# Moving w_out's weight conversion from the attention to the matrix groups, and batching the softmax sums by three

## Chip, cores and metric

One core of one Trainium2 chip. The metric is the device time of one execution, in microseconds. Three runs of the kernel before took 563.81, 565.52 and 565.93 us, median 565.52.

## What is computed

Attention with a relative bias, then a layer of three matrix products with an elementwise maximum, and an output product. 4 batches, 8 heads, 576 positions, 64 columns a head; 2304 tokens, 512 columns, 768 hidden columns.

```python
scores = scale * q @ k.T + bias[head, i, j]
attn = exp(scores - max(scores)); attn = attn / (sum(attn) + 1e-9)
x = (attn @ v) as 2304 x 512
h = maximum(maximum(x @ w1, x @ w2), x @ w3)     # 512 x 768 each
out = h @ w_out                                   # 768 x 512
```

The reference's `moe` weights are float64: each weight reaches the chip as two 32-bit words, and the kernel makes float32 of them.

## The kernel before, in words

**Bias** (lines 93 to 180): a table of biases is made and written to DRAM; the attention reads it back per head pair and tile of rows.

**Attention** (class `Attention`, loop at line 1197 of the program). 16 units (head pair and batch) make 8 pairs of units, and each pair has nine steps, so there are 72 steps; `sched` is the order of the transposes, `fronts` that of the scores (the same but for the first pair, in which the fourth tile is scored sixth). A step's number modulo nine is called its place. `step(n)` issues, in this order: the scores of step n on TensorE (`front`, 12 matmuls of 288 columns in float32r, of two heads side by side); one to three pairs of output products (`pv`); on VectorE one `shift` per head (line 285: scores and bias, scale, and the row's minimum as negative maximum); on ScalarE one exponential per head with the row's sum (line 298), and an addition of 1e-9 to the two sums (line 302); VectorE's copies of finished outputs (line 402); the stream's VectorE token; then `norm(n-1)`: a reciprocal on VectorE (line 307) and the normalisation of both heads on GpSimd (line 310); `flip(n-5)`: the transposes of the step five back on TensorE (line 337), whose results ScalarE (lines 428, 429) and VectorE (line 431) copy out; the splits of the next units' queries and keys into a high and a low part (ScalarE line 239, GpSimd line 242). The score banks are two buffers, so a front waits for the shifts of the step before it. Engines run in the order in which the program issues.

**The stream of conversions** (`first`, lines 1103 to 1165; `convert`, line 540). One conversion makes 128 x 512 float32 of the word pairs: one operation on ScalarE (line 545) and four on VectorE (lines 547, 549, 552, 555). It is a generator of tokens, "scalar" or "vector"; from step 8 on each step but those at place 0 lets it do one VectorE token (two at places 1 and 3) and, at the step's end, one ScalarE token if that is next. Converted in this stream are sets 3 and 2 of the first three weights (each set two conversions), then w_out's three blocks (two conversions each, tiles `w64o` and `wao`), then sets 0 and 1. Sets 3, 2 and w_out's blocks get four GpSimd sums each and are written to `w_d` in DRAM with their sums, two stores of 512 KB a block. All loads and stores are on SP's queue, one after the other. A second stream (`early_x`) prepares parts of x from step 36 on.

**Matrix stage** (`moe`). First a plain stage for set 0, then groups 3 to 26: eight sets of weights by three column blocks, seven products a group (a Strassen-like scheme). Set s works in groups 3s to 3s+2. Products are made in the order p5, p6, p2, p7, the next group's p1, p4, p3; ahead of each there is a slot, 0 to 6, in which the jobs placed by `at(group, slot, ...)` are issued. ScalarE copies p1, p6 and p7 out of the bank in which the next product goes on; VectorE makes the sums of p2, p7 and p3 and, except in every third set, a running maximum of 128 x 384 and one of 128 x 1152 a group. Sets 4 to 8 are converted here, one token a job (`advance`), ten tokens in three groups from group 4 on. `raise_w` and `lower_w` split the weights on ScalarE and GpSimd. Groups 27 to 35 are the output products; their weights `wop` are loaded from `w_d` at groups 21 to 23 (`load_wo`, line 812) and split by `raise_wo` (ScalarE, line 827; the first of them, p3, in group 22, slot 2) and `lower_wo`.

Of the kernel before, what the change touches and what calls it, by code (L numbers as in the profile page):

```python
# [9 lines left out]
F32 = mybir.dt.float32  # L10
F32R = mybir.dt.float32r
U32 = mybir.dt.uint32
ACTF = mybir.ActivationFunctionType
ALU = mybir.AluOpType
# [5 lines left out]
def kernel(  # L20
# [12 lines left out]
    nc = tc.nc  # L33
# [10 lines left out]
    KFF = DFF // 128  # L44
# [152 lines left out]
    NS = len(STEPS)  # L197
# [2 lines left out]
    fronts = [sched[x] for x in (0, 1, 2, 4, 5, 3)] + sched[6:]  # L200
    NSTEP = len(sched)
    LAG = 5
    EB = LAG + 2
    GW = 128 * 2

# [3 lines left out]
    class Attention:  # L209
        def __init__(self, pool):  # L210
            self.pool = pool
            self.data = {}
            self.st = {}
            self.et = {}
            self.pvq = []
            self.done = []
            bias_t.extend(pool.tile([128, 2, S], F32, name=f"bias{t}", bufs=1) for t in range(NTQ + 1))
            self.vl = [pool.tile([128, 2, D], F32, name=f"vl{x}", bufs=1) for x in range(2)]
            for x in self.vl:
                nc.gpsimd.memset(x, 0.0)  # L220
# [70 lines left out]
        def expo(self, n, h):  # L291
            pool, st = self.pool, self.st[n]
            if h == 0:
                st["e"] = pool.tile([128, 2 * S], F32, tag=f"e{sched.index(fronts[n]) % (LAG + 1)}", bufs=1,
                                    name=f"e{n}")
                st["sm"] = pool.tile([128, 2], F32, tag="sm", bufs=EB, name=f"sm{n}")
            sn, nm = st.pop(h)
            nc.scalar.activation(st["e"][:, S * h:S * h + S], sn, ACTF.Exp, scale=-1.0, bias=nm,  # L298
                                 accum_out=st["sm"][:, h:h + 1])
            if h:  # L300
                sm = st["sm"]
                nc.scalar.activation(sm, sm, ACTF.Copy, bias=1e-9)

        def norm(self, n):
            st = self.st[n]
            rc = self.pool.tile([128, 2], F32, tag="rc", bufs=EB, name=f"rc{n}")
            nc.vector.reciprocal(rc, st["sm"])  # L307
            for h in range(2):
                e = st["e"][:, S * h:S * h + S]
                nc.gpsimd.tensor_scalar(out=e, in0=e, scalar1=rc[:, h:h + 1], scalar2=1.0,  # L310
                                        op0=ALU.mult, op1=ALU.mult)

        def group(self, un, g):
# [90 lines left out]


        def step(self, n, more=()):
            m, f = n - 1, n - LAG
            if n < NSTEP:
                pair, y = fronts[n]
                which, t = step_of(pair, y)  # L410
# [83 lines left out]
    def arith(eng, out, a, b, op=ALU.subtract):  # L494
        f = lambda x: x.bitcast(F32) if x.dtype == F32R else x
        eng.tensor_tensor(out=out, in0=f(a), in1=f(b), op=op)  # L496
# [37 lines left out]
    def fetch(pool, srcs, name):  # L534
        w = pool.tile([128, 512, 2], U32, tag="w64", bufs=2, name=f"w64{name}")
        n = 512 // len(srcs)
        for x, src in enumerate(srcs):
            nc.sync.dma_start(out=w[:, n * x:n * x + n].rearrange("p (c f) t -> p c (f t)", c=src.shape[1]), in_=src)
        return w

    def convert(pool, w, out, name):
        a = pool.tile([128, 512], F32, tag="wa", bufs=1, name=f"wa{name}")
        high, low, t = w[:, :, 1], w[:, :, 0], a.bitcast(U32)
        yield "scalar"
        nc.scalar.activation(a, high.bitcast(F32), ACTF.Abs, scale=2.0 ** 16)
# [46 lines left out]
    def moe(pool, wpool, x0, xa, xb, raw, sr):  # L592
# [89 lines left out]
        def at(n, k, *what):  # L682
            jobs.setdefault((n, k), []).extend(what)
# [84 lines left out]
        sumgen = {}  # L768

        fetched = {}  # L770

        def get(s, d):
            fetched[s, d] = fetch(wpool, w_srcs(s, d), f"{s}_{d}")

        def work_w():
            for s in range(4, NSET):
                made_w[s] = [raw_tile(pool if s % 2 == 0 else wpool, s), None]
                for d in range(2):
                    if d == 0:
                        get(s, 1)  # L780
                    elif s + 1 < NSET:
                        get(s + 1, 0)
                    yield from convert(wpool, fetched.pop((s, d)),
                                       made_w[s][0][:, 512 * d:512 * d + 512].bitcast(U32), f"{s}_{d}")

        ww = work_w()
        started = []
# [4 lines left out]
            next(ww, None)  # L792

        at(2, 0, F(get, 4, 0))
        for s in range(4, NSET):
            n = 3 * s - 8
            for k in range(10):
                at(n + (0, 0, 0, 0, 1, 1, 1, 2, 2, 2)[k], (2, 4, 5, 6, 2, 4, 6, 2, 4, 6)[k], advance)

        wo = {}  # L800
        wst = {}
# [222 lines left out]
    with tc.manual_schedule():  # L1024
# [45 lines left out]

        def first():
            todo = [(w_srcs(s, d), f"{s}_{d}") for s in PARK for d in range(2)]
            todo += [(wo_srcs(i + d * KFF // 2), f"o{i}_{d}") for i in range(KFF // 2) for d in range(2)]
            todo += [(w_srcs(s, d), f"{s}_{d}") for s in range(2) for d in range(2)]
            ahead = [fetch(wpool, *todo.pop(0))]

# [35 lines left out]

            for _ in range(2):
                yield "vector"
            parked = [(f"{s}", s - PARK[1]) for s in PARK] + [(f"o{i}", 2 + i) for i in range(KFF // 2)]
            for name, k in parked:
                made, half = block(name)
                for d in range(2):
# [47 lines left out]
        while n < NSTEP + LAG:  # L1166
            more = []
            if n >= NS - 1 and n % NS:
                more += [w0] * (2 if n % NS in (1, 3) else 1)
            if n >= 36 and n % NS in (3, 7, 8):  # L1170
                more.insert(0, ex)
            if n >= NSTEP + 1:
                more.insert(0, lx)
            at.step(n, more)
            n += 1
# [61 lines left out]
```

## Time and profile before

| | |
|---|---|
| median of three runs | 565.52 us |
| the profiled execution | 564.47 us, its span 562.70 us |
| busy in the span | TensorE 538.5 us (96%), VectorE 448.5 (80%), ScalarE 367.6 (65%), GpSimd 284.1 (50%) |
| bias table, first steps | to about 76 us |
| attention steps 9 to 71 | 75.85 to 276.30 us |
| last transposes, x's parts | to about 300 us |
| matrix groups and output | 300 to 562.7 us |
| granted TensorE clock | 1.00 in all slices (2.4 GHz) |
| DMA | 80.75 MB, SP's queue 45.2% of the 16 engines' span |

In a view of windows a line gives the window, its length, then for PE (matmuls), PEld (weight loads), DVE (VectorE), ACT (ScalarE) and POOL (GpSimd) the busy time with the number of instructions, then the granted clock, the DMA's busy share and GB/s. In a timeline a line gives start and duration in us, engine, line of the code, operation, result and operands, and in brackets the engine's idle time before it with what ended it.

### The profile page before, as it was taken

The numbers are of one execution on the slowest core, as the hardware profiler recorded it, in microseconds if no ns is written. First come the engines' busy times: TensorE is split into PE (matmuls) and PEld (weight loads), VectorE is DVE, ScalarE is ACT, GpSimd is POOL, SyncE is SP. The second block draws the span as 40 slices with busy tenths as digits, with TensorE's granted clock in tenths as the row PEclk, the third lists the DMA queues.
The fourth block names the chain that finished last, engine by engine and source line by source line (L and its number), as shares of the span: only waits on it lengthen the run. The fifth ranks groups of instructions, "written<-read, shape, count | busy, mean of one in ns | idle before, by whom it ended". The sixth has DMA issues, their size and how long they took to land.

```text
span 562.7 us, 13799 instructions
## 1 busy us (share of the span) xinstructions
PE 538.5 (96%) x5239; PEld 443.6 (79%) x5239; DVE 448.5 (80%) x949; ACT 367.6 (65%) x850; POOL 284.1 (50%) x296
## 2 busy tenths in 40 slices
PE   8999899999999899999889999999999999999997
PEld 4455666666666666666569999999999999999997
DVE  7996779999999999999668786754776237798883
ACT  6997798989899888898756643234323334445552
POOL 0637577788787989787620136344364242600000
PEclk9999999999999999999999999999999999999999
DMA  4895963944694457431200422421125300557552
GB/s 137 230 336 169 365 199 99 363 134 162 183 337 139 147 143 215 153 101 23 61 1 1 150 67 76 147 91 44 47 94 167 123 29 29 166 179 211 176 169 76
DMA packets 73170, 80.75 MB, mean 144 GB/s; under 512 B 23120, under 2 KB 54096, under 8 KB 73104
## 3 DMA queue, kind: packets, MB, share of 16 engines
q1 hardware_dynamic: 72960, 79.58, 45.2%
q8 instruction: 41, 0.67, 0.5%
q10 hardware_dynamic: 144, 0.29, 0.2%
q14 instruction: 25, 0.20, 0.1%
HBM read 50.61 MB, written 28.99 MB: 141 GB/s over the span
## 4 chain that ended last, share of the span: by engine, by line
PE 68%; ACT 13%; DVE 10%; issue 4%; DMA 2%; POOL 1%; SPq 0%; ACTq 0%; DVEq 0%; POOLq 0%
PE p L606 10%; PE p L604 10%; PE p L605 10%; ACT e L298 6%; PE pv L383 6%; PE bp L134 5%; PE s L275 5%; DVE sn L285 4%; PE p_o L950 4%; PE p_o L949 4%; PE p_o L948 4%; ACT et L428 2%; PE tp L337 2%; DVE et L431 2%; PE c L604 2%
## 5 line engine op out<-in xcount | busy, mean ns | idle before, releaser
L310 POOL TENSOR_SCALAR e<-e,rc 128x576 f32<-128x576 f32 x144 | 112.8, 796 | 40.4 <-DVE rc L307 37.3
L298 ACT ACTIVATE e<-sn,nm 128x576 f32<-128x576 f32 x144 | 111.4, 774 | 23.1 <-DVE nm L285 21.6
L285 DVE CUSTOM_DVE_ANT_0 sn<-s,bias 128x576 f32<-128x576 f32 x144 | 102.7, 748 | 11.9 <-PE s L275 8.9
L383 PE MATMUL pv<-et,vt 128*64 128x320 f32 (+1 forms) x496 | 74.0, 418 | 3.9 <-ACT et L428 2.2
L496 POOL TENSOR_TENSOR wl<-wr,wh 128x256 fp32r<-128x256 f32 x25 | 23.0, 946 | 94.2 <-ACT wh L692 94.2
L275 PE MATMUL s<-kh,qh 64*128 64x288 f32 x256 | 58.5, 337 | 5.5 <-DVE nm L285 4.7
L431 DVE COPY et<-tp 128x512 f32<-128x512 f32 x72 | 48.4, 672 | 10.7 <-PE tp L337 5.7
L337 PE MATMUL tp<-ident,e 64*128 64x64 f32 x1152 | 55.4, 226 | 0.5 <-DVE et L431 0.4
L383 PEld LDWEIGHTS pv<-et,vt 128*64 128x64 f32 x496 | 32.4, 136 | 27.1 <-issue 6.7
L644 ACT COPY u<-p 128x384 f32<-128x384 f32 x24 | 11.5, 479 | 59.3 <-PE p L606 59.1
L275 PE MATMUL s<-kl,qh 64*128 64x288 f32 x256 | 49.2, 303 | 0.0
L337 PEld LDWEIGHTS lp<-ident,e 64*128 64x128 f32 x144 | 19.7, 137 | 36.6 <-issue 17.3
L275 PE MATMUL s<-kh,ql 64*128 64x288 f32 x256 | 46.3, 290 | 0.9 <-POOL ql L242 0.9
L428 ACT COPY et<-tp 128x512 f32<-128x512 f32 x72 | 41.2, 572 | 7.7 <-PE lp L337 5.3
L337 PEld LDWEIGHTS tp<-ident,e 64*128 64x128 f32 x1152 | 45.3, 139 | 0.9 <-DVE et L431 0.9
L242 POOL TENSOR_TENSOR kl<-kr,kh 128x576 fp32r<-128x576 f32 x16 | 36.5, 2280 | 16.6 <-ACT kh L239 16.5
L275 PEld LDWEIGHTS s<-kh,qh 64*128 64x128 f32 x256 | 35.2, 186 | 12.0 <-DVE nm L285 9.6
L134 PE MATMUL bp<-hid,w2s 128*32 128x79 f32 (+51 forms) x640 | 41.9, 406 | 2.5 <-DVE hid L113 1.4
L113 DVE TENSOR_SCALAR hid<-sm,bp 128x528 f32<-128x528 f32 (+17 forms) x108 | 41.4, 458 | 0.0
L337 PE MATMUL lp<-ident,e 64*128 64x64 f32 x144 | 35.4, 246 | 5.2 <-ACT et L429 5.0
L134 PEld LDWEIGHTS bp<-hid,w2s 128*32 128x32 f32 x640 | 20.6, 114 | 24.3 <-issue 16.8
L496 POOL TENSOR_TENSOR wl<-ws,wh 128x256 fp32r<-128x256 f32 x28 | 27.5, 1008 | 14.6 <-ACT wh L694 11.9
(230 smaller groups left out, 1650.5 us busy)
## 6 DMA issues: line engine op xcount, KB each, us to landing
bias_d<-bs SPq DMA_DIRECT2D x36, 295.5 KB, 5.5
bias<-bias_d SPq DMA_DIRECT2D x16, 576.0 KB, 6.6
w<-in_moe_w_dram SPq DMA_DIRECT2D x36, 256.0 KB, 3.5
h_d<-ht SPq DMA_DIRECT2D x18, 384.0 KB, 3.7
hin<-h_d SPq DMA_DIRECT2D x16, 384.0 KB, 4.6
qr<-in_qd_dram SPq DMA_DIRECT2D x16, 288.0 KB, 4.9
kr<-in_kd_dram SPq DMA_DIRECT2D x16, 288.0 KB, 5.2
vt<-in_v_dram SPq DMA_DIRECT2D x32, 128.0 KB, 3.6
```

The lines of the kernel that those rows point to most:

```text
L134: nc.tensor.matmul(bp[32 * c:32 * c + 32, o:o + w], lhsT=w2s, rhs=src, start=True, stop=True)
L275: nc.tensor.matmul(ss[h][:, x, 0:HALF], lhsT=u[q][p, 128 * t:128 * t + 128], rhs=u[k][p, cols], start=(j == 0), stop=(j == 2))
L285: nc.vector.tensor_tensor_reduce(out=sn.rearrange("p (a b) -> p a b", a=2), in0=st["s"][h][:, :, 0:HALF], in1=bt.rearrange("p (a b) -> p a ...
L298: nc.scalar.activation(st["e"][:, S * h:S * h + S], sn, ACTF.Exp, scale=-1.0, bias=nm, accum_out=st["sm"][:, h:h + 1])
L310: nc.gpsimd.tensor_scalar(out=e, in0=e, scalar1=rc[:, h:h + 1], scalar2=1.0, op0=ALU.mult, op1=ALU.mult)
L337: return nc.tensor.transpose(to, e2[p, k0:k0 + 128], ident[p, p])
L383: nc.tensor.matmul(pv[p], lhsT=w, rhs=x, start=(c == 0), stop=(c == NTQ))
L428: nc.scalar.copy(*tp0[0])
L431: nc.vector.tensor_copy(*x)
L604: nc.tensor.matmul(o, lhsT=hi[:, c], rhs=h[:, j], start=first and j == 0, stop=False, **on)
L605: nc.tensor.matmul(o, lhsT=hi[:, c], rhs=l[:, j], start=False, stop=False, **on)
L606: nc.tensor.matmul(o, lhsT=lo[:, c], rhs=h[:, j], start=False, stop=last and j == 1, **on)
```

## The change

w_out's blocks leave the attention's stream. In the matrix stage the conversions come in one order, set 4's two halves, w_out's first half-block, set 5's two, and so on, the last two of w_out at the end, one conversion a group from group 4 to 19 (w_out's in groups 6, 9, 12, 15, 18, 19), one token in each of slots 1, 2, 4, 5 and 6. The four sums of a block follow in the next group on GpSimd, with four stores in place of two. In the attention the stream gets one VectorE token a step at every place but 0. The sums of three steps share one tile, one addition and one reciprocal, so normalisation n is issued in step n+3 in place of n+1.

```diff
+    BATCH = 3
 def expo(self, n, h):
-                st["sm"] = pool.tile([128, 2], F32, tag="sm", bufs=EB, name=f"sm{n}")
+                if n % BATCH == 0:
+                    self.sm = pool.tile([128, 2 * BATCH], F32, tag="sm", bufs=3, name=f"sm{n}")
             sn, nm = st.pop(h)
+            x = 2 * (n % BATCH) + h
             nc.scalar.activation(st["e"][:, S * h:S * h + S], sn, ACTF.Exp, scale=-1.0, bias=nm,
-                                 accum_out=st["sm"][:, h:h + 1])
-            if h:
-                sm = st["sm"]
-                nc.scalar.activation(sm, sm, ACTF.Copy, bias=1e-9)
+                                 accum_out=self.sm[:, x:x + 1])
+            if x == 2 * BATCH - 1:
+                nc.scalar.activation(self.sm, self.sm, ACTF.Copy, bias=1e-9)
+                self.sums.append(self.sm)
 def norm(self, n):
-            rc = self.pool.tile([128, 2], F32, tag="rc", bufs=EB, name=f"rc{n}")
-            nc.vector.reciprocal(rc, st["sm"])
+            if n % BATCH == 0:
+                self.rc = self.pool.tile([128, 2 * BATCH], F32, tag="rc", bufs=3, name=f"rc{n}")
+                nc.vector.reciprocal(self.rc, self.sums.pop(0))
 def step(self, n, more=()):
-            m, f = n - 1, n - LAG
+            m, f = n - BATCH, n - LAG
...
 in moe:
+        order = []
+        for s in range(4, NSET):
+            order += [(s, 0), (s, 1), ("o", s - 4)]
+        order.append(("o", NSET - 4))
+            if d % 2 == 0:
+                stage[d // 2] = [pool.tile([128, 768], F32, tag="st", bufs=3, name=f"wos{d}_{x}") for x in range(3)]
+            return stage[d // 2][d % 2][:, 0:512]
         def work_w():
+            for k, x in enumerate(order):
+                if k + 1 < len(order):
+                    get(*order[k + 1])
+                yield from convert(wpool, fetched.pop(x), halves(*x).bitcast(U32), f"{x[0]}_{x[1]}")
+        def sum_wo(b, k):
+            r0, r1, r2, r3 = (stage[b][x // 2][:, 256 * (x % 2):256 * (x % 2) + 256] for x in range(4))
+            to = [stage[b][2][:, 256 * x:256 * x + 256] for x in range(3)] + [stage[b][0][:, 512:768]]
+            x, y, op = ((r0, r2, ALU.add), (to[0], r1, ALU.subtract), (r1, r0, ALU.subtract),
+                        (r3, to[1], ALU.subtract))[k]
+            arith(g, to[k], x, y, op)
+            if k == 0:
+                for x in range(2):
+                    nc.sync.dma_start(out=w_d[2 + b, 0, :, 512 * x:512 * x + 512], in_=stage[b][x][:, 0:512])
+            elif k == 2:
+                nc.sync.dma_start(out=w_d[2 + b, 1, :, 0:768], in_=stage[b][2])
+            elif k == 3:
+                nc.sync.dma_start(out=w_d[2 + b, 1, :, 768:1024], in_=stage[b].pop(0)[:, 512:768])
-        for s in range(4, NSET):
-            n = 3 * s - 8
-            for k in range(10):
-                at(n + (0, 0, 0, 0, 1, 1, 1, 2, 2, 2)[k], (2, 4, 5, 6, 2, 4, 6, 2, 4, 6)[k], advance)
+        for x in range(len(order)):
+            for k in (1, 2, 4, 5, 6):
+                at(4 + x, k, advance)
+            if order[x][0] == "o" and order[x][1] % 2:
+                for k, y in enumerate((2, 3, 4, 6) if x + 1 < len(order) else (0, 1, 2, 3)):
+                    at(5 + x, y, F(sum_wo, order[x][1] // 2, k))
 in first:
-            todo += [(wo_srcs(i + d * KFF // 2), f"o{i}_{d}") for i in range(KFF // 2) for d in range(2)]
-            parked = [(f"{s}", s - PARK[1]) for s in PARK] + [(f"o{i}", 2 + i) for i in range(KFF // 2)]
+            parked = [(f"{s}", s - PARK[1]) for s in PARK]
 in the loop of steps:
-                more += [w0] * (2 if n % NS in (1, 3) else 1)
+                more += [w0]
```

## Rows read from the trace of the kernel before

**Rows 1.** Windows by stage: two of the attention, one of the matrix groups

```profile
75.85:206.78 130.93, 124.70 (x1614) 83.86 (x1614) 128.52 (x326) 117.95 (x322) 106.89 (x118) 1.00 0.59 185
206.78:276.30 69.52, 65.35 (x856) 44.31 (x856) 65.34 (x167) 61.74 (x171) 57.04 (x67) 1.00 0.42 120
...
342.00:445.00 103.00, 103.00 (x594) 103.00 (x593) 62.21 (x95) 34.87 (x65) 48.32 (x55) 1.00 0.32 107
```

**Rows 2.** Windows of single steps, at places 1, 5, 6 and 7

```profile
251.85:255.28 3.43, 3.43 (x45) 2.27 (x46) 2.87 (x9) 3.37 (x12) 2.16 (x4) 1.00 0.00 0
...
265.95:268.41 2.46, 2.46 (x39) 1.85 (x34) 2.20 (x8) 1.62 (x5) 2.17 (x4) 1.00 0.03 7
268.41:271.09 2.68, 2.68 (x41) 1.98 (x42) 2.50 (x9) 2.54 (x9) 1.28 (x2) 1.00 0.25 56
271.09:273.68 2.59, 2.59 (x40) 1.95 (x42) 2.22 (x7) 2.53 (x8) 2.59 (x5) 1.00 0.28 62
```

**Rows 3.** Timeline of VectorE from 257 us on

```profile
257.11 0.15 DVE L307 RECIPROCAL rc<-sm 128x2 f32<-128x2 f32 x1
257.18 0.67 DVE L431 COPY et<-tp 128x512 f32<-128x512 f32 x1
257.76 0.71 DVE L547 TENSOR_SCALAR wa<-wa 128x512 f32<-128x512 f32 x1
258.40 0.74 DVE L285 CUSTOM_DVE_ANT_0 sn<-s,bias 128x576 f32<-128x576 f32 x1
...
259.75 1.55 DVE L549 TENSOR_SCALAR wa<-wa 128x512 uint32<-128x512 uint32 x1
```

**Rows 4.** Windows of steps 9 to 71, conversions (VectorE, ScalarE): w_out's, others

```profile
75.85:276.30 200.45, 22.92 (x24) 4.20 (x6) 1.00 0.53 163
...
75.85:276.30 200.45, 31.92 (x32) 5.56 (x8) 1.00 0.53 163
```

**Rows 5.** Windows of steps 9 to 71, line 307 alone (VectorE)

```profile
75.85:276.50 200.65, 9.58 (x64) 1.00 0.53 162
```

**Rows 6.** Windows of steps 9 to 71, line 302 alone (ScalarE)

```profile
75.85:276.30 200.45, 12.73 (x63) 1.00 0.53 163
```

**Rows 7.** Waits from 110 to 260 us: us in total, times, longest

```profile
POOL e L310 <- DVE rc L307: 16.6, 19, 1.3
ACT e L298 <- DVE nm L285: 11.6, 14, 2.3
```

**Rows 8.** Timeline of GpSimd at step 8

```profile
73.56 1.41 POOL L242 TENSOR_TENSOR ql<-qr,qh 128x576 fp32r<-128x576 f32 x1
74.95 1.47 POOL L310 TENSOR_SCALAR e<-e,rc 128x576 f32<-128x576 f32 x2
```

**Rows 9.** Timeline of TensorE at step 8

```profile
75.03 0.40 PE L275 MATMUL s<-kh,ql 64*128 64x288 f32 x2 [0.89 <-POOL ql L242]
```

**Rows 10.** Windows of the matrix groups, conversion tiles alone (VectorE, ScalarE)

```profile
345.00:445.00 100.00, 23.87 (x34) 5.38 (x8) 1.00 0.33 110
```

**Rows 11.** Timeline of VectorE in a matrix group with a running maximum

```profile
351.74 0.56 DVE L496 TENSOR_TENSOR q<-p,u 128x384 f32<-128x384 f32 x1 [1.00 <-ACT u L651]
...
353.18 0.43 DVE L549 TENSOR_SCALAR wa<-wa 128x512 uint32<-128x512 uint32 x1
...
355.17 1.36 DVE L496 TENSOR_TENSOR ht<-ht,q 128x1152 f32<-128x1152 f32 x1
...
357.47 0.56 DVE L496 TENSOR_TENSOR q<-p,m 128x384 f32<-128x384 f32 x1 [0.28 <-PE p L606]
358.98 0.56 DVE L496 TENSOR_TENSOR q<-p,u 128x384 f32<-128x384 f32 x1 [0.95 <-ACT u L651]
```

**Rows 12.** DMA issues: count, KB each, us to landing

```profile
wop<-w_d SPq DMA_DIRECT2D x7, 384.0 KB, 5.9
```

**Rows 13.** Line 827: duration in ns, first and last start in us

```profile
L827 ACT CAST woh<-wop x3: 827/837/839, 459.1 to 471.8; 128x768 fp32r<-128x768 f32 x3
```

**Rows 14.** Timeline of GpSimd at 259 us

```profile
259.60 1.41 POOL L242 TENSOR_TENSOR ql<-qr,qh 128x576 fp32r<-128x576 f32 x1 [0.52 <-ACT qh L239]
```

More of the change, by code (lines that the diff above doesn't have):

```diff
@@ L216, in __init__ @@
             self.done = []
+            self.sums = []
             bias_t.extend(pool.tile([128, 2, S], F32, name=f"bias{t}", bufs=1) for t in range(NTQ + 1))
@@ L295, in expo @@
                                     name=f"e{n}")
-                st["sm"] = pool.tile([128, 2], F32, tag="sm", bufs=EB, name=f"sm{n}")
+                if n % BATCH == 0:
+                    self.sm = pool.tile([128, 2 * BATCH], F32, tag="sm", bufs=3, name=f"sm{n}")
             sn, nm = st.pop(h)
+            x = 2 * (n % BATCH) + h
             nc.scalar.activation(st["e"][:, S * h:S * h + S], sn, ACTF.Exp, scale=-1.0, bias=nm,
-                                 accum_out=st["sm"][:, h:h + 1])
-            if h:
-                sm = st["sm"]
-                nc.scalar.activation(sm, sm, ACTF.Copy, bias=1e-9)
+                                 accum_out=self.sm[:, x:x + 1])
+            if x == 2 * BATCH - 1:
+                nc.scalar.activation(self.sm, self.sm, ACTF.Copy, bias=1e-9)
+                self.sums.append(self.sm)
         def norm(self, n):
             st = self.st[n]
-            rc = self.pool.tile([128, 2], F32, tag="rc", bufs=EB, name=f"rc{n}")
-            nc.vector.reciprocal(rc, st["sm"])
+            if n % BATCH == 0:
+                self.rc = self.pool.tile([128, 2 * BATCH], F32, tag="rc", bufs=3, name=f"rc{n}")
+                nc.vector.reciprocal(self.rc, self.sums.pop(0))
             for h in range(2):
                 e = st["e"][:, S * h:S * h + S]
-                nc.gpsimd.tensor_scalar(out=e, in0=e, scalar1=rc[:, h:h + 1], scalar2=1.0,
+                x = 2 * (n % BATCH) + h
+                nc.gpsimd.tensor_scalar(out=e, in0=e, scalar1=self.rc[:, x:x + 1], scalar2=1.0,
                                         op0=ALU.mult, op1=ALU.mult)
@@ L770, in moe @@
         fetched = {}
-        def get(s, d):
-            fetched[s, d] = fetch(wpool, w_srcs(s, d), f"{s}_{d}")
-        def work_w():
-            for s in range(4, NSET):
[L777 to L784, printed above, removed]
+        order = []
@@ new lines, in moe, with halves @@
+        for s in range(4, NSET):
+            order += [(s, 0), (s, 1), ("o", s - 4)]
+        order.append(("o", NSET - 4))
+        stage = {}
+        def get(s, d):
+            srcs = w_srcs(s, d) if s != "o" else wo_srcs(d // 2 + d % 2 * KFF // 2)
+            fetched[s, d] = fetch(wpool, srcs, f"{s}_{d}")
+        def halves(s, d):
+            if s != "o":
+                if d == 0:
+                    made_w[s] = [raw_tile(pool if s % 2 == 0 else wpool, s), None]
+                return made_w[s][0][:, 512 * d:512 * d + 512]
+            if d % 2 == 0:
+                stage[d // 2] = [pool.tile([128, 768], F32, tag="st", bufs=3, name=f"wos{d}_{x}") for x in range(3)]
+            return stage[d // 2][d % 2][:, 0:512]
@@ L794, in moe @@
         at(2, 0, F(get, 4, 0))
-        for s in range(4, NSET):
-            n = 3 * s - 8
-            for k in range(10):
-                at(n + (0, 0, 0, 0, 1, 1, 1, 2, 2, 2)[k], (2, 4, 5, 6, 2, 4, 6, 2, 4, 6)[k], advance)
+        for x in range(len(order)):
[4 more added lines that the diff above has]
+                    at(5 + x, y, F(sum_wo, order[x][1] // 2, k))
         wo = {}
```

## The prediction

> **What bounds the kernel now.** I read the page's slices first, then busy time by stage, then single steps. The stage table [rows 1] shows two regimes. In the attention (steps 9 to 71, 75.85 to 276.30 us, 63 steps of 3.18 us) VectorE is busy for 128.52 of 130.93 us and then 65.34 of 69.52 us. In the matrix groups TensorE is busy for 103.00 of 103.00 us, while VectorE works 62.21, ScalarE 34.87 and GpSimd 48.32. So time taken off VectorE counts in the attention, and the same work may be free in the groups.
>
> TensorE's 95% in the attention must not be read as a bound. Its records hold modelled tails, and steps without any conversion run shorter with the same kind of matmuls: 2.46, 2.68 and 2.59 us [rows 2]. In these the two shifts release the score banks, the next front runs, and the next shift starts. The exception is the step at place 1 of every nine (3.43 us): VectorE works 2.87 of it, one conversion operation included, and idles the rest, so that place has a floor of its own.
>
> A step with conversions is longer by what they take. The step behind that one, from 255.28 to 258.40 us, lasts 3.12 us and holds one operation that pushes the next shift from 257.76 to 258.40 us, 0.64 us [rows 3]. VectorE goes from operation to operation without a gap there.
>
> **Part 1: conversions leave the attention.** They are 24 VectorE operations of 22.92 us, 0.955 us each, and six on ScalarE of 4.20 us; the 32 that stay take 31.92 us [rows 4]. Records overlap by some 0.07 us, so I charge 0.90 us an operation. The stream gets one VectorE slot a step where it had two at places 1 and 3, and the shortened list ends at step 53 where it ended at step 71; its last VectorE conversion is in step 49.
>
> I worked it out step by step, as the longer of a floor and VectorE's sum. VectorE's work without conversions is, by place 0 to 8, 2.45, 2.03, 2.50, 2.01, 2.50, 2.02, 2.39, 2.02 and 2.02 us: step lengths less the conversions' start-to-start time, for instance 3.12 - 0.64 = 2.48 at place 2 [rows 3]. A check from the totals: 200.45 us, less 6.6 us idle [rows 1], less 54.84 x 0.93 for conversions without their overlap [rows 4], is 142.9 us over 63 steps or 2.27 a step, against a mean of 2.22. The floors are 2.45, 3.43, 2.50, 2.60, 2.54, 2.46, 2.66, 2.59 and 2.65 us; places 1, 5, 6 and 7 are in rows 2, the others are my choice between the last three of those values, since most of these steps never ran bare, and place 0 is as long as its own work. For the program before, this gives 196.6 us against 200.45 measured, 2% short.
>
> For the changed one, steps 9 to 49 go from 129.8 to 123.4 us: 32 of 41 steps carry one operation, and the five at place 1 hide it. Steps 50 to 71 run at their floors: 66.8 to 58.1 us. Together **-15.1 us**, the reciprocals of part 2 included. With operations of 0.57 us, my estimate of an undisturbed one between the 0.43 of rows 11 and the 0.70 of rows 10, it would be -23; with 1.2 us each, -6.2; with every floor 0.15 us higher, -9.6.
>
> **Part 2: 48 reciprocals and 48 additions go.** A reciprocal takes 9.58 / 64 = 0.150 us [rows 5], but the copy behind it starts 0.07 us after its start [rows 3], so one is worth 0.08 us at most, and nothing where a floor holds: 1.5 us in all, inside the sum above. An addition is 12.73 / 63 = 0.20 us of ScalarE [rows 6]. ScalarE waits for VectorE's shifts [rows 7], so I take zero; if ScalarE led, 48 would be worth up to 9.6 us, and that is in the lower end only. The batch's reciprocal stands in a step whose number divides by three and reads sums finished in the step before, as every reciprocal did, so VectorE waits no more than now.
>
> **Part 3: the normalisation comes two steps later.** It is issued two steps ahead of its transposes instead of four. GpSimd waits for reciprocals now [rows 7]; afterwards two of three normalisations start as soon as GpSimd is free. It works 57.04 of 69.52 us [rows 1], 2.6 us a step of which conversions' sums are a part that partly goes, so two steps of lead cover it, with one exception. The fourth tile of the first pair stands at place 5 of the front order, so its normalisation is issued in step 8 itself, just ahead of its transposes, and behind the query split on GpSimd. That split ran from 73.56 us, the next normalisation from 74.95 to 76.42 us [rows 8]. TensorE's next front waited for the split until 75.03 us [rows 9]; now the transposes and that whole front come behind 76.42 us: 1.4 us more, and some 0.6 by estimate for the transposes and the front's head, which ran ahead of that wait. **+2 us**, once (0 if VectorE makes it up, 3 at most).
>
> **Part 4: conversions in groups 6 to 19.** Each group gets a whole conversion, one operation at each of slots 1, 2, 4, 5 and 6. There a VectorE operation took 23.87 / 34 = 0.70 us [rows 10], so 24 are 17 us, in groups whose VectorE is free for 40 of 103 us [rows 1]. The tight groups are the nine with a running maximum: four operations of 0.56, one of 1.36 and four conversions of 0.70 make 6.4 of the 7.24 us between two groups' same copies. One such stretch exists already: from 351.74 to 358.98 us VectorE did just this, idling 0.28 + 0.95 us [rows 11], and TensorE's stage has no gap [rows 1]. GpSimd gets 12 short additions in 55 idle us of this stage [rows 1], and behind them stand low parts of weights that TensorE needs a group later. Price: **0**, bounds -0.5 and +4.
>
> SP loses six fetches and six stores in the attention and gets the fetches and 12 smaller stores in the groups. A fetch still waits for the last conversion operation ahead of it, and the stores of h queue behind. The last quarter of the third block is added in group 20 and fetched again at the head of group 21, so SP waits there for GpSimd and a store, and four more fetches wait behind. A load lands in 5.9 us [rows 12], and its cast on ScalarE, in slot 2 of group 22, ran at 459.1 us [rows 13]. Two groups of 7.24 us earlier and a slot later, at 445.6, the addition is issued; with 1.5 us for it and its queue, and a store as long as the load, the data is there by 458.9 at the latest. Past 459.1 ScalarE waits, and behind it the copies that free TensorE's banks: 0, at most +3.
>
> **Sum.** -15.1 + 2 = -13.1 against the profiled execution's 564.47 us (span 562.70 and 1.77 around it): 551.4. The median of the runs, 565.52, lies 1.05 above that execution; I take **552.0**.
>
> **A rule weighed.** At 259.75 us an operation (line 549) took 1.55 us [rows 3] that took 0.43 at 353.18 [rows 11]; GpSimd's split ran from 259.60 to 261.01 us [rows 14], and the operation ended 0.3 us after it. The Trainium skill, page "SBUF — State Buffer", section "SBUF: two separate sides", says that VectorE (with two SBUF inputs or in a two-port mode) and GpSimd hold one port pair in turn, a whole instruction long. By that rule the operation would end 0.43 us behind the split; the trace agrees within 0.15 us. It speaks against both parts; what it would make of them is rival 2.
>
> **Rivals.**
> 1. *The floor is nearer than I think.* Floors come from single steps between slower ones, where ScalarE and TensorE could catch up. In a row of nine they may be 0.15 to 0.3 us higher: -9.6 to -3.7, with the start 557 to 563. For: ScalarE works 89% of the second stretch [rows 1]. Against: three bare steps in a row (265.95 to 273.68) stay at 2.46 to 2.68, with VectorE idle for 0.18 to 0.37 us of each [rows 2].
> 2. *GpSimd blocks more.* After a batch reciprocal, three normalisations of 1.47 us [rows 8] can follow each other, and a conversion in the next two steps meets one. At 1.2 us an operation: -6.2 + 2, 560. Against: GpSimd's total falls, and steps that divide by three get free of it. (The skill's page above is the rule behind this one.)
> 3. *Slower: VectorE becomes the bound of the nine groups with a running maximum.* Its sum is 3.6 us plus four conversions against 7.24 us. At 0.91 us an operation it fills the group; at 1.27 the excess of 9 x 1.44 us eats the gain; at 1.5 it is 9 x 2.36 = 21 us and 573. For: the attention's operations took 0.955. Against: 34 of them in this stage took 0.70, and the full group of rows 11 kept up.
> 4. *The change does less than it says*: conversions that stay cost more steps than I count because fewer slots are given. The list still ends 18 steps earlier, so I give this 1 in 50, no change.
>
> **How the numbers follow.** Forecast 0.69 (545 to 557), rival 1 0.16, rival 2 0.08, rival 3 0.05, rival 4 0.02. The low end is undisturbed operations (-23 + 2, 543.5, rounded up, as not all will be), the high end rivals 1 and 2: 545 to 560. What a measurement can tell from no change is 0.5%, 2.8 us. Faster: the forecast and most of rivals 1 and 2, 0.87; same 0.07; slower 0.06.
>
> **What would show it.** Right: steps 9 to 49 at about 3.0 us each and steps 50 to 71 at 2.65 to 2.75, where VectorE idles before shifts; a step 8 longer by 2 us; groups 6 to 19 unchanged at TensorE 100%. Wrong: conversions of over 1.1 us in either stage (rivals 2, 3), bare steps of 2.9 us (rival 1), TensorE waiting for a sum by VectorE in groups 6 to 19, ScalarE waiting for the cast in group 22, or transposes that wait for GpSimd in the steady state.

## The result, and the profile after

The changed kernel took 558.12 us (median of 4 runs, 557.74 to 561.19), the kernel before beside it 565.72 (563.81 to 566.75): ratio of the means 0.988, with a 95% interval of [0.984, 0.993]. It is faster by 7.6 us by the medians and by 6.7 by the means, and the time lies in the range; but 13.5 us had been forecast (13.1 against the profiled execution), so about half of the gain did not come. What came is rival 1, which gave 557 to 563 us.

To find the place, the span is cut at the first shift of a step on VectorE (one step runs to the next step's first shift):

| part of the span, us | before | after | difference | forecast |
|---|---|---|---|---|
| up to step 0 | 51.26 | 50.43 | -0.8 | |
| steps 0 to 8 | 24.59 | 27.64 | +3.05 | +2 |
| of these, step 8 | 4.23 | 6.81 | +2.58 | +2 |
| steps 9 to 49 | 130.93 | 128.14 | -2.8 | -6.4 |
| steps 50 to 70 | 66.89 | 60.63 | -6.3 | -8.7, with step 71 |
| step 71 to the end | 289.02 | 289.16 | +0.1 | 0 |
| span | 562.70 | 556.00 | -6.7 | -13.1 |

The start up to step 0 holds nothing that was edited and differs from one execution to the next.

First the windows of the stages after, in the columns of [rows 1]: steps 9 to 49, steps 50 to 70, and the matrix groups; the fourth line is the same stretch of the matrix groups with w_out's conversion tiles alone (VectorE, ScalarE).

```profile
78.07:206.20 128.13, 123.26 (x1618) 83.19 (x1618) 118.32 (x291) 114.38 (x296) 104.67 (x114) 0.99 0.51 152
206.20:266.84 60.64, 59.67 (x827) 41.75 (x824) 48.32 (x131) 53.91 (x143) 46.71 (x56) 1.00 0.37 103
335.00:438.00 103.00, 103.00 (x594) 103.00 (x593) 77.32 (x116) 39.02 (x70) 62.17 (x65) 1.00 0.42 142
...
335.00:438.00 103.00, 16.90 (x24) 3.36 (x5) 1.00 0.42 142
```

In the second line VectorE's busy time has fallen to 48.32 of 60.64 us, and TensorE's matmuls fill 59.67 of it. In the third, TensorE is still busy for all 103.00 us although VectorE's work rose from 62.21 to 77.32 us and GpSimd's from 48.32 to 62.17 [rows 1]; w_out's 24 operations take 16.90 us, 0.70 each.

The waits from 85 to 260 us (us in total, times, longest), first of the kernel before, then after, show what is late now.

```profile
PEld lp L337 <- POOL e L310: 1.9, 4, 0.5
...
DVE sn L285 <- PE s L275: 1.0, 5, 0.2
```

```profile
PEld lp L343 <- POOL e L316: 5.8, 9, 1.1
...
DVE sn L287 <- PE s L277: 5.3, 18, 0.3
DVE sn L287 <- PE s L270: 3.2, 6, 0.5
```

VectorE's shifts waited for TensorE's scores 5 times for 1.0 us, now 24 times for 8.5 us; and transposes wait for GpSimd's normalisations 9 times instead of 4. The first is the floor. The second is only in part the batch: run 1 below, which has no batch, shows 8 such waits for 3.7 us, but none over 0.5 us.

**Steps without conversions.** Steps 54 to 70 hold none. Windows of four of them, at places 1, 3, 5 and 7, in the columns of [rows 2]:

```profile
219.57:222.98 3.41, 3.41 (x44) 2.25 (x46) 2.13 (x5) 3.27 (x10) 3.32 (x5) 1.00 0.42 162
225.76:229.34 3.58, 3.58 (x48) 2.02 (x47) 2.24 (x6) 3.51 (x10) 2.68 (x4) 1.00 0.18 42
232.19:235.23 3.04, 3.04 (x44) 2.30 (x43) 2.13 (x6) 3.01 (x9) 1.84 (x2) 1.00 0.05 14
237.70:240.62 2.92, 2.87 (x41) 2.16 (x42) 2.14 (x7) 2.83 (x8) 2.92 (x5) 1.00 0.26 61
```

VectorE works 2.13 to 2.24 us in each, and the step lasts 2.92 to 3.58. The chain of waits (start, us, what) says why: here it runs on TensorE alone, one piece directly behind the other; over steps 55 to 70 (219.56 to 266.83 us) TensorE has 92% of it. First the shares by line of that stretch, then the pieces about place 5.

```profile
by line: PE pv L389 40.7%; PE s L277 23.9%; PE tp L343 15.9%; PE lp L343 6.7%; PE s L270 4.8%; ACT e L302 3.5%; issue 2.3%; ACT et L434 1.0%; ACT sm L305 0.4%; ACT et L435 0.4%; DVE sn L287 0.2%; DVE nm L287 0.2%; DVEq L287 0.1%; ACTq L302
```

```profile
230.49 0.20 PE lp L343
230.70 0.50 PE tp L343 x16
231.20 0.84 PE s L277 x12
232.04 1.49 PE pv L389 x12
233.53 0.20 PE lp L343
233.74 0.50 PE tp L343 x15
234.24 0.84 PE s L277 x12
235.08 1.01 PE pv L389 x8
```

From 232.04 to 235.08 us are the output products, transposes and next scores of one step: 1.49 + 0.70 + 0.84 = 3.03 us, against 3.04 measured at place 5. The other places follow in the same way, with output products of 1.0 to 1.8 us and scores of 0.84 to 0.98, or 1.13 where they mix two batches.

**Step 8.** One line of TensorE's timeline, then the windows about it (columns as in [rows 1]):

```profile
75.54 0.27 PE L343 MATMUL lp<-ident,e 64*128 64x64 f32 x1 [3.41 <-POOL e L316]
```

```profile
75.50:77.00 1.50, 1.46 (x25) 1.47 (x26) 0.69 (x1) 0.59 (x2) 0.00 (x0) 0.70 0.90 197
77.00:79.00 2.00, 2.00 (x14) 0.97 (x14) 0.94 (x3) 0.23 (x2) 0.00 (x0) 0.50 0.99 335
79.00:81.00 2.00, 2.00 (x32) 1.73 (x34) 1.79 (x6) 1.83 (x5) 0.87 (x2) 0.87 0.39 137
```

The transposes waited 3.41 us for GpSimd's normalisation, as part 3 said. Then the granted clock was 0.70 and 0.50 on average (1.2 in place of 2.4 GHz for 3.4 us, from 76.1 us on); that was in no term.

### The profile page after: what moved, and what is told of

Same layout as the page of the kernel before. It is cut to its first block, busy times and chain, and to the rows that moved or that the text cites. A ratio compares the mean times of both kernels' runs of the same rounds, so it can differ in the third digit from the quotient of the medians.

```text
span 556.0 us, 13725 instructions
## 1 busy us (share of the span) xinstructions
PE 533.3 (96%) x5239; PEld 442.4 (80%) x5239; DVE 439.3 (79%) x901; ACT 361.6 (65%) x802; POOL 295.1 (53%) x296
## 4 chain that ended last, share of the span: by engine, by line
PE 75%; ACT 7%; POOL 6%; DVE 5%; issue 4%; DMA 2%; SPq 1%; POOLq 0%; DVEq 0%; ACTq 0%
PE p L610 10%; PE p L612 10%; PE p L611 10%; PE pv L389 9%; PE bp L134 6%; PE s L277 5%; ACT e L302 4%; PE p_o L982 4%; PE p_o L981 4%; PE p_o L980 4%; PE tp L343 4%; POOL e L316 3%; PE lp L343 2%; PE c L610 2%; PE c L612 2%
## 5 line engine op out<-in xcount | busy, mean ns | idle before, releaser
L316 POOL TENSOR_SCALAR e<-e,rc 128x576 f32<-128x576 f32 x144 | 111.6, 795 | 37.3 <-DVE rc L312 29.3
L277 PE MATMUL s<-kh,qh 64*128 64x288 f32 x256 | 53.4, 339 | 3.1 <-DVE nm L287 2.5
L244 POOL TENSOR_TENSOR kl<-kr,kh 128x576 fp32r<-128x576 f32 x16 | 41.3, 2580 | 25.4 <-ACT kh L241 24.6
L277 PE MATMUL s<-kl,qh 64*128 64x288 f32 x256 | 45.7, 300 | 0.0
L277 PE MATMUL s<-kh,ql 64*128 64x288 f32 x256 | 43.9, 292 | 0.0
L277 PEld LDWEIGHTS s<-kh,qh 64*128 64x128 f32 x256 | 32.1, 189 | 7.2 <-DVE nm L287 5.4
L502 POOL TENSOR_TENSOR wl<-ws,wh 128x256 fp32r<-128x256 f32 x28 | 29.4, 1074 | 14.3 <-ACT wh L700 11.6
```

The costliest lines, as they stand in the source:

```text
L277: nc.tensor.matmul(ss[h][:, x, 0:HALF], lhsT=u[q][p, 128 * t:128 * t + 128], rhs=u[k][p, cols], start=(j == 0), stop=(j == 2))
L316: nc.gpsimd.tensor_scalar(out=e, in0=e, scalar1=self.rc[:, x:x + 1], scalar2=1.0, op0=ALU.mult, op1=ALU.mult)
```

## The experiments

Ten kernels ran. Theory T: beyond VectorE's work a step is bounded by TensorE's sequence, nearer than my floors; the gain ends there, and the batch adds nothing but step 8. Against it stood that the lost gain is a loss by the batch (L), or that the conversions left in the attention, stretched by GpSimd, hold it (F). Parts in us, cut as above, each from one execution; "start" is the first shift of step 0. The ratio is that of the means, with its 95% interval, to runs of the kernel before that were taken beside the run in question; runs 4, 5, 6 and 8 ran once, so only their parts are read.

| kernel | time (runs) | ratio to before | start | 0 to 8 | 9 to 49 | 50 to 70 | 71 to end |
|---|---|---|---|---|---|---|---|
| before | 565.72 (4) | | 51.26 | 24.59 | 130.93 | 66.89 | 289.02 |
| after | 558.12 (4) | 0.988 [0.984, 0.993] | 50.43 | 27.64 | 128.14 | 60.63 | 289.16 |
| 1 move only | 554.45 (4) | 0.982 [0.980, 0.984] | 51.24 | 24.63 | 127.72 | 59.96 | 289.36 |
| 2 batch only | 564.79 (10) | 1.000 [0.998, 1.002] | 51.25 | 28.43 | 129.59 | 65.79 | 287.84 |
| 3 three together | 553.65 (5) | 0.980 [0.978, 0.982] | 50.69 | 25.30 | 125.53 | 60.53 | 289.14 |
| 4 no VectorE conversion | 558.86 (1) | | 53.26 | 28.13 | 123.24 | 61.79 | 290.68 |
| 5 two terms, before | 560.63 (1) | | 50.19 | 22.60 | 131.39 | 65.65 | 288.97 |
| 6 two terms, after | 550.53 (1) | | 51.04 | 26.49 | 123.00 | 58.84 | 289.34 |
| 7 free places | 555.47 (5) | 0.984 [0.981, 0.986] | 51.37 | 25.32 | 124.86 | 63.16 | 290.69 |
| 8 matrix twice | 569.06 (1) | | 50.59 | 25.32 | 126.61 | 60.52 | 304.26 |
| 9 five places | 554.51 (6) | 0.983 [0.980, 0.987] | 51.26 | 25.30 | 123.66 | 61.77 | 290.61 |
| 10 five places, single | 551.39 (5) | 0.978 [0.975, 0.980] | 54.22 | 25.15 | 121.82 | 61.90 | 289.41 |

**1. The move without the batch.** The changed kernel with one step to a batch:

```diff
-    BATCH = 3
+    BATCH = 1
-                    self.sm = pool.tile([128, 2 * BATCH], F32, tag="sm", bufs=3, name=f"sm{n}")
+                    self.sm = pool.tile([128, 2 * BATCH], F32, tag="sm", bufs=EB, name=f"sm{n}")
-                self.rc = self.pool.tile([128, 2 * BATCH], F32, tag="rc", bufs=3, name=f"rc{n}")
+                self.rc = self.pool.tile([128, 2 * BATCH], F32, tag="rc", bufs=EB, name=f"rc{n}")
```

> The changed kernel with the sums of each step on their own again (one addition, one reciprocal a step, normalisation n issued in step n+1): the move of w_out's conversions alone. Theory T (after the move TensorE's own sequence sets the steps: 26.3 us per nine steps at the end of the attention, whatever VectorE and GpSimd do): steps 50 to 71 as in the changed kernel, within 1 us (63.2 us for the 22); step 8 back to about 4.2 us from 6.8 and no clock drop behind it, worth 3 us; the 28 reciprocals more in steps 9 to 49 cost 1 to 2 us. Together 556 to 557. Rival L (the floor is 23.9 us per nine steps, as predicted, and the shorter lead of the normalisations holds the steps above it): with the lead of four steps back, steps 50 to 71 fall to 58 us and the whole to 550 to 552.

554.45 us. Steps 50 to 70 take 59.96 us, as after (60.63), with 21 reciprocals and 21 additions where after has 7: L falls. The 14 additions of 0.20 us on ScalarE that after saves in these steps shorten nothing either. The kernel is about 2 us better than T said, and 3.7 faster than after: between the spans (3.1 us) steps 0 to 8 give 3.0, of which step 8 gives 2.6, steps 9 to 70 another 1.1, and a later start takes 0.8 back. In the chain of steps 55 to 70 ScalarE has a third here (TensorE two thirds) at the same length, 46.99 us against 47.27 after: the two floors lie close together.

**2. The batch without the move.** The kernel before with the hunks of `expo`, `norm` and `m = n - BATCH` alone:

```diff
-    m, f = n - 1, n - LAG
+    m, f = n - BATCH, n - LAG
```

> The kernel before with the batching of the sums alone, w_out's conversions left in the attention. T: VectorE still sets the steps, so 48 reciprocals less give 1.5 to 2.5 us, and the late normalisation in step 8 costs 2.6 us there and some 1 us by the clock behind it: 565.5 to 568, no change to the kernel before within what can be told. Rival L (the short lead costs in every step): slower by 5 us or more, 570 and up.

564.79 us, no difference from before, a little under T's figure; L falls. The accounts are two: steps 9 to 70 are 2.4 us shorter, the reciprocals part 2 gave 1.5 for; steps 0 to 8 are 3.8 us longer. Step 8 makes some 2 of these (6.28 us against 4.23), with TensorE waiting 2.88 us for the same normalisation. Step 6 makes 1.0 (3.65 us against 2.61): there the granted clock was at half from 67.5 to 70.9 us, which after and run 3, with the same batch, do not show (2.49 us), so this part is not shown to be the batch's. With VectorE relieved as well the 2.4 us are not there in after: from run 1 to after, steps 9 to 70 get 1.1 us longer. In run 3, which has the batch too, they are 1.6 us shorter than in run 1.

**3. The row of three issued at once.** The changed kernel; when the reciprocal of three steps is there, all three normalisations are issued behind it:

```diff
-            if 0 <= m < NSTEP:
-                self.norm(m)
+            if 0 <= m < NSTEP and m % BATCH == 0:
+                for k in range(BATCH):
+                    self.norm(m + k)
```

> The changed kernel with the three normalisations of a batch issued together in the step of their reciprocal, so the second and third come one and two steps earlier. T: only step 8 (and the clock drop behind it) gets better, 6.8 to about 4.2 us: 554 to 555.5, steps 50 to 71 at 62 to 64 us. Rival L: steps 50 to 71 fall as well, to 58 to 60 us, and the whole to 549 to 552.

553.65 us, 4.5 us better than after and a little better than T said, which had only step 8 get better. Step 8 takes 4.47 us, and steps 9 to 49 lose 2.6 us: the four conversion operations issued at place 5 take 0.99 us each instead of 1.69, and their four steps are 2.8 us shorter. Over all 32 operations the mean falls only from 0.83 to 0.81, as those at place 3 take 0.98 instead of 0.48. Where an operation is stretched counts: by the bare steps and VectorE's sums, place 3 has room for 3.57 - 2.01 = 1.56 us of it, place 5 for 3.04 - 2.02 = 1.02 (an estimate).

**4. No conversion on VectorE in the attention.** The changed kernel; in the attention's stream all four VectorE operations and the ScalarE one go, and one ScalarE operation writes the tile instead, so the weights are not converted:

```diff
-                for token in convert(wpool, ahead.pop(0), out, name):
+                for token in convert_short(wpool, ahead.pop(0), out, name):
...
+        nc.scalar.activation((out() if callable(out) else out).bitcast(F32), w[:, :, 1].bitcast(F32), ACTF.Abs)
```

> The changed kernel without the four VectorE operations of each conversion that is left in the attention (its weights are then not the inputs' weights; ScalarE writes the tile with one operation instead). T: all steps from 9 on fall to TensorE's 2.92 us, so steps 9 to 71 (start to start) take 180 to 183 us instead of 188.8, and the whole 550 to 552. Rival F (the floor is 23.9 us per nine steps): 165 to 170 us, and the whole 536 to 540.

Its first step began 2.8 us late, before anything edited, and the whole, 558.86 us, lies far above what T gave; the parts are read and not the whole. Windows of steps 9 to 49 and 50 to 70, columns as above:

```profile
81.56:204.80 123.24, 118.73 (x1618) 80.88 (x1616) 96.78 (x260) 112.99 (x293) 97.69 (x114) 0.99 0.51 153
204.80:266.60 61.80, 59.93 (x830) 41.80 (x828) 48.62 (x130) 54.85 (x146) 46.95 (x56) 1.00 0.36 102
```

VectorE is down to 96.78 of 123.24 us, and the 62 steps still take 185.0 us against 188.8 after: taking away all that was left of the conversions gave 3.8 us, where F asked for 19 to 24 us. It ends 2 us above T's 180 to 183. This is the floor nearly by itself: 185.0 / 62 = 2.98 us a step, where I had taken 23.88 / 9 = 2.65. From step 55 on there is nothing else: these 16 steps take 47.27 us after, 47.30 in run 3 and 47.26 here.

**5 and 6. Less work on TensorE, before and after.** Two of the three products of each score are issued, in either kernel:

```diff
-            terms = (("qh", "kh"), ("qh", "kl"), ("ql", "kh"))
+            terms = (("qh", "kh"), ("qh", "kl"))
...
-                                         rhs=u[k][p, cols], start=(j == 0), stop=(j == 2))
+                                         rhs=u[k][p, cols], start=(j == 0), stop=(j == 1))
```

> The kernel before with two of the three score products (the low part of the queries is left out of the scores), so TensorE has four matmuls, some 0.28 us, less in 64 of the 72 steps. T (before the change VectorE sets the steps that carry conversions): steps 50 to 70 fall by 0 to 2.5 us from 66.9, steps 9 to 49 by 0 to 4 from 130.9. Rival (TensorE set them already): both fall by the full 0.25 us a step, 5.2 and 10 us.

> The changed kernel with two of the three score products (the same part left out). T (TensorE's sequence sets the steps once the conversions are gone): steps 50 to 70 fall by 4 to 6 us from 60.6, since seven of nine places are TensorE's; steps 9 to 49, in which conversions remain, by 2 to 6 from 128.1. Rival G (GpSimd's late normalisation sets them): steps 50 to 70 stay within 1.5 us of 60.6.

Before, steps 9 to 70 change by -0.8 us: TensorE did not set them. After, the same cut takes 5.1 us from steps 9 to 49, and 1.8 from steps 50 to 70, fewer than T's 4 to 6 and just above the 1.5 of rival G (GpSimd's late normalisation). Run 1 speaks against G: without the late normalisation these steps take 59.96 us against 60.63. So TensorE's sequence became the bound; but close behind it lies the next, less than 0.1 us a step (1.8 / 21) by this run. With the cut, the chain of steps 50 to 70 changes between TensorE's output products (28%), ScalarE's exponentials (10%) and GpSimd.

**7. Conversions only where VectorE waits.** From step 10 to 67 VectorE tokens go out at places 1, 5 and 7, and two at place 3, on top of run 3:

```diff
-                more += [w0]
+                more += [w0] * (2 if n % NS == 3 else 1)
+            w0.hold = n % NS not in (1, 3, 5, 7) and 10 <= n < 68
```

> The changed kernel with the three normalisations of a batch together, and the conversions' VectorE operations let in only at the places where TensorE is the longer one: one at places 1, 5 and 7, two at place 3; the list then lasts until step 75 instead of 53. The same work, spread. T: nearly all of them vanish under TensorE's 2.92 us a step, so steps 9 to 49 fall from 125.5 to 120 to 122 us, steps 50 to 70 rise by at most 1 from 60.5, and the whole is 548.5 to 551. Rival F (every conversion costs its length wherever it stands): steps 9 to 49 gain what steps 50 to 70 lose, 553 to 554.

555.47 us, 2 us worse than run 3, and above what either theory gave. At places 1 and 7 the operations vanished: those steps took 3.46 and 2.98 us on average against 3.43 and 2.92 bare. At 3 and 5 they took 1.13 and 1.26 us on average, up to 2.1, and did not fit. Neither theory holds whole. With five operations in nine steps the list also runs on to step 71, so steps 50 to 70 are longer than in run 3.

**8. Doubled conversions in the matrix groups.** Run 3 with three of the four VectorE operations issued twice in the groups, for rival 3:

```diff
-                yield from convert(wpool, fetched.pop(x), halves(*x).bitcast(U32), f"{x[0]}_{x[1]}")
+                yield from convert_twice(wpool, fetched.pop(x), halves(*x).bitcast(U32), f"{x[0]}_{x[1]}")
```

> The changed kernel with the normalisations together, and three of the four VectorE operations of each conversion in the matrix groups issued twice (the second time with the same result): some 2.2 us more of VectorE in each of groups 4 to 19. T: a group with a running maximum needs 6.4 + 2.2 = 8.6 us of VectorE against 7.24 us of TensorE, so TensorE waits there, 1.2 to 1.6 us in each of groups 5 to 8 and 12 to 17, while groups 9 to 11, 18 and 19 stay: the time from the start of step 71 to the end grows from 289.1 by 8 to 16 us. Rival (the cover is wider, VectorE may lag a group behind): it grows by less than 4.

The part from step 71 on is 15.1 us longer than in run 3, inside the 8 to 16 expected. Windows of the groups, run 3 and then this one:

```profile
331.00:434.00 103.00, 103.00 (x593) 103.00 (x593) 77.03 (x116) 38.54 (x69) 62.15 (x65) 1.00 0.42 139
```

```profile
331.00:449.00 118.00, 107.82 (x597) 102.75 (x596) 110.80 (x161) 38.50 (x71) 65.74 (x62) 1.00 0.37 124
```

With VectorE at 110.80 of 118.00 us TensorE idles for 10.2. The mechanism of rival 3 is real, and only the slack kept the move free.

**9 and 10. One conversion operation at each of five places**, 1, 3, 5, 7 and 8, on top of run 3 (9), and the same with one step to a batch (10):

```diff
+            w0.hold = n % NS not in (1, 3, 5, 7, 8)
```

> As the run with the free places, but one VectorE operation at each of places 1, 3, 5, 7 and 8 (place 3 with one in place of two). There the second operation at place 3 made that step 4.2 to 4.5 us and pushed the reciprocal and the normalisations into the key split, so that the operation at place 5 took 2.0 us. T with the contention: one operation at place 3 (up to 1.5 us) and one at place 5 (0.75 to 1.3) hide under TensorE, at place 8 it costs 0.2. Steps 9 to 49 at 121 to 123.5 us (124.9 with two at place 3, 125.5 with one at every place), steps 50 to 70 at 61 to 62.5, the whole 551 to 553. Rival F (what counts is the number of operations in the stage, not their place): 184 to 186 us for steps 9 to 70 as in both others, the whole 553.5 to 555.5.

> The same five places with the sums of each step on their own (no batch, normalisation n in step n+1): GpSimd gets one normalisation a step and no row of three. T with the contention: TensorE's floor again, less stretched operations, but a reciprocal more in six of nine steps, which costs 0.08 us only at places 2, 4 and 6: 551 to 553.5, within 1 us of the batched one. If the row of three normalisations is what stretches the operations, this one is faster by 1 us or more.

The list runs to step 70 in both. Run 9 does not tell the two theories apart by its parts: steps 9 to 70 take 185.4 us, which F's 184 to 186 holds and the sum of T's parts, 182 to 186, as well; the whole, 554.51 us, lies in F's range and not in T's. Run 10 takes 551.39 us, the best of all, and 3.1 us less than run 9, which differs from it by the batch alone; 1 us or more was what the expectation asked for, if the row of three normalisations stretches the operations. The mean conversion operation in run 10 is 0.72 us, in run 9 0.87. So with this schedule the batch does stretch them. With the schedule of the changed kernel it does not: their mean is 0.83 after and 0.83 in run 1 (before: 0.98), and only the places differ.

How they are stretched shows in step 23, first in the timelines of VectorE and of GpSimd after:

```profile
122.74 2.00 DVE L561 SCALAR_TENSOR_TENSOR wr<-w,signm,wa 128x512 uint32<-128x512 uint32 x1
```

```profile
119.46 3.35 POOL L316 TENSOR_SCALAR e<-e,rc 128x576 f32<-128x576 f32 x4
122.77 1.42 POOL L244 TENSOR_TENSOR kl<-kr,kh 128x576 fp32r<-128x576 f32 x1
```

then in those of run 9, in the same step, with another operation of a conversion:

```profile
120.02 1.83 DVE L562 SCALAR_TENSOR_TENSOR wa<-w,wa 128x512 uint32<-128x512 uint32 x1
```

```profile
119.87 1.43 POOL L244 TENSOR_TENSOR kl<-kr,kh 128x576 fp32r<-128x576 f32 x1 [0.25 <-ACT kh L241]
```

and in those of run 10, with the same operation as in run 9:

```profile
122.18 0.69 DVE L562 SCALAR_TENSOR_TENSOR wa<-w,wa 128x512 uint32<-128x512 uint32 x1
```

```profile
120.24 1.47 POOL L316 TENSOR_SCALAR e<-e,rc 128x576 f32<-128x576 f32 x2 [1.29 <-DVE rc L312]
122.38 1.78 POOL L244 TENSOR_TENSOR kl<-kr,kh 128x576 fp32r<-128x576 f32 x1 [0.67 <-ACT kh L241]
```

After, four normalising instructions, one behind the other (119.46 to 122.81), put the key's split off to 122.77, where it meets the operation that begins with it. Run 1, without the batch, has four in a row in the same step too:

```profile
117.11 3.45 POOL L316 TENSOR_SCALAR e<-e,rc 128x576 f32<-128x576 f32 x4
```

So that row is not the batch's doing. In run 9 the split began 0.15 us ahead of the operation, which ended 0.55 us behind it; in run 10 the operation began 0.2 us ahead of the split, took 0.69 us, and the split was the one that grew, from 1.42 to 1.78. So the operation is short where it comes first, and in both runs what the split waited for last was not GpSimd's normalisations but ScalarE's cast of the key (0.25 and 0.67 us). That it is GpSimd's row of three that stretches the operations is thus not shown in this step; why the cast comes later without the batch was not followed up.

## Why the prediction was half right

**What failed is a term of part 1, the floors.** The step that reads: places 1, 5, 6 and 7 "are in rows 2, the others are my choice between the last three of those values". The bare steps after, by place 0 to 8, last 2.57, 3.43, 2.77, 3.57, 2.86, 3.04, 2.47, 2.92 and 2.58 us (means of two, at place 0 the second, at place 8 the one), 26.21 for nine, where I had 23.88: 0.26 us a step, inside the 0.15 to 0.3 of rival 1. Of the 2.33 us, 1.6 lie at the places that I chose (0, 2, 3, 4 and 8), 0.97 of them at place 3 alone, and 0.7 at those that I read. The method itself stood, more or less: with these floors the same rule (floor or VectorE's sum, the longer) gives about 198 us for steps 9 to 70 of before, measured 197.83, and about 189 after, measured 188.77. With mine it gives 193.9 and 178.8. That it comes so near is partly luck: for run 1 the rule gives 190 and for run 3 about 189, measured 187.68 and 186.06, as it charges 0.90 us an operation wherever one stands. The warning was there: for before, mine came out 2% short.

The single steps misled me because they spent time that had been saved before them. In front of 265.95 us, where my three bare steps begin, stood steps of 4.20 and 3.35 us, of which VectorE was busy for 4.17 and 3.35; TensorE had got ahead, waited for it in the second, and gave the time back in the bare ones. The chain of before shows it:

```profile
265.31 1.51 PE pv L383 x12
266.82 0.20 PE lp L337
267.03 0.50 PE tp L337 x16
267.52 0.00 PE lp L337
267.53 0.96 PE s L275 x12
```

That is 3.17 us of TensorE's pieces in a step that I read as 2.46, place 5. They began 0.64 us ahead of the step's shift at 265.95, while after the same pieces began 0.15 us ahead (232.04 and 232.19). After has rows of nine with nothing saved. "Against: three bare steps in a row" was thus no evidence against rival 1, which had named just this: steps "between slower ones, where ScalarE and TensorE could catch up".

Floors nearer the true ones stood in the chain of before, one view further on. Part of a step at place 1, and scores, output products and transposes around a step at place 3:

```profile
251.93 1.76 PE pv L383 x12
253.69 0.20 PE lp L337
253.90 0.50 PE tp L337 x16
254.40 0.00 PE lp L337
254.40 0.84 PE s L275 x12
```

```profile
229.44 1.83 PE pv L383 x12
231.27 0.20 PE lp L337
231.48 0.50 PE tp L337 x14
231.98 1.23 PE s L268 x16
```

1.76 + 0.70 + 0.84 = 3.30 us at place 1 (3.43 after); 1.83 + 0.70 + 1.23 = 3.76 at place 3 (3.57 after), for which I had 2.60. The sentence "TensorE's 95% in the attention must not be read as a bound" was right of steps 9 to 49 before (run 5), and wrong as a reason to leave TensorE's own sum out. The Trainium skill, page "Perfetto Trace Analysis", section "Identifying the Most-Contended Engine", holds matmul busy time to be no good measure of how close TensorE is to its roofline, and names the matmul FLOPs against the peak (MFU) and the weight loads' busy share in its place. No run here gives the first. In steps 50 to 70 after, weight loads fill 41.75 of 60.64 us (69%), ScalarE is busy for 53.91 (89%) and matmuls for 59.67 (98%), while TensorE has 92% of the chain from step 55 on. So here the weight loads' share would have put TensorE behind ScalarE, and the chain puts it first.

**Operations of 0.90 us**: right in size before (0.98 with overlap), 0.83 after.

**Part 2**: 1.5 us was right in kind for the kernel before (run 2: 2.4), and nothing is seen of it in after, whose steps 9 to 70 are longer than run 1's. Zero for the additions held.

**Part 3**: the mechanism and its place were right, +2.58 for step 8 against +2. Its price left out the granted clock. "Two steps of lead cover it" failed in part: transposes wait for GpSimd 9 times for 5.8 us, up to 1.1, where they waited 4 times, and run 1 has 8 waits for 3.7 us. Rival 2 came in small: the mean of all operations is no longer than in run 1 (0.83 us in both), but at place 5, where there is little room, it is 1.69 against 1.16.

**Part 4**: right throughout. The groups took the 24 operations of 0.70 us at no cost. The cast of p3, for whose data I had left up to 3 us, waited for nothing and ran at 452.26 us, 6.8 earlier than before [rows 13], as the whole stage does (ScalarE's timeline):

```profile
452.26 0.84 ACT L859 CAST woh<-wop 128x768 fp32r<-128x768 f32 x1
```

**What stays open.** All parts rest on single executions, and stretches of about 3.4 us at half clock fall into different parts from one to the next: runs 4, 7, 9 and 10 have one near 270 us as well, and in runs 4, 7 and 9 the part from step 71 on is 1.5 us longer than in run 3. Differences of about 1 us between parts are thus not told apart. Run 10's first step was late by about 3 us in its profiled execution (554.27 us), so how its gain of 2.3 us on run 3 splits by part rests on that one execution. That steps 50 to 70 are 1.3 us longer in run 4 than in run 3, with no VectorE conversion in either, lies in steps 50 to 54 alone and was not followed up. And rival 2 was tested only as far as runs 3, 9 and 10 go: GpSimd's splits, which stretch operations too, stayed in every run. No run made ScalarE's exponentials or its copies shorter, so how near ScalarE's own floor lies is known only from run 6.

## What to carry to other kernels

When a busy engine is relieved, find the floor below it by adding up the next engine's in-order pieces for each place of the pattern, from the chain; a single short step behind a long one may spend what was saved in that one. Work moved under an engine that is busy for all of a stage is free as long as the slack lasts, and then costs (0 us for 24 operations; 15.1 us for run 8, with some 34 us more of VectorE's work). Batching small operations that gate another engine moves the time at which the released work starts: here it paid to issue all of it at once, or not to batch; moving without the batch was worth 3.7 us more than with it.

## What the hardware showed that I had not expected

TensorE's granted clock fell to half for about 3.4 us at the end of step 8, after waits of 3.41 us (after) and 2.88 us (run 2). The length of the wait is not the whole of it: runs 3 and 8 have the same attention and the same wait of 0.97 and 0.96 us there, and run 8 shows such a fall from 76.3 us on and run 3 none. Run 2 shows another in step 6, from 67.5 us on, inside a wait of 0.90 us; run 3 waits 0.89 us at the same point without one. Between runs 3 and 8 it costs 1.0 us: steps 9 and 10 take 3.18 + 3.83 us in run 8 and 2.46 + 3.55 in run 3.

A VectorE operation whose record begins 0.03 us ahead of a GpSimd split (122.74 and 122.77) ended 0.55 us behind the split's end, 2.00 us in place of some 0.7 (0.75 for the same operation in run 10, step 32): beginning first by so little did not save it here, while a lead of 0.2 us did in run 10.
